# Order of the opening's transposes on TensorE, and of their copies on VectorE, in a fused layer-norm, linear-attention and gated-MLP kernel

## The chip, the cores and the metric

The kernel runs on one core of one Trainium2 chip. The metric is device time in microseconds (us). Where a ratio is given, it is the mean time of one kernel's runs over that of the other's runs of the same rounds, so it is not quite the ratio of the medians beside it.

## The reference, cut to what matters

```python
x = A_x                                   # 2048 x 640, bf16
xn = _layernorm(x, axis=-1)
return x + _A_ref(xn, A_wqkv, A_w_phi, A_wo) + _B_ref(xn, B_w1, B_w3, B_w2)
# _A_ref: q, k, v = xn @ wqkv; softmax feature maps of q and k; kv state; out @ wo
# _B_ref: (silu(xn @ w1) * (xn @ w3)) @ w2
```

Everything starts from the normalized rows xn, and the matmuls of this kernel read them transposed, with the contraction index on the partitions.

## The kernel before

The 2048 rows are 16 tiles of 128. Tiles 0 to 3 are the opening: they are transposed on TensorE (PE), and the later tiles by DMA. For each of the four tiles VectorE (DVE) computes mean and variance and writes a normalized (or, at first, only centered) tile; PE transposes its five 128x128 blocks into one or two PSUM banks; ScalarE (ACT) or DVE copies them to xnT; and PE multiplies xnT by wv (ten matmuls of 320 columns per tile: "V" below).

Tiles 0 and 1 are transposed twice. The first time they are only centered, so that V can start before the variance is known, and ACT multiplies V by the reciprocal standard deviation when it empties the accumulators. The second time they are fully normalized, for all later readers of xnT. Those later readers are first the "gate" matmuls (512 columns, with w1 and w3), which need all four tiles. The start of the first gate matmul is thus the end of the opening.

```python
def T(t, lo, hi, evac, dep, after=()):       # transposes of blocks lo..hi of tile t; cut
    def fn():
        o["ps"] = bank([P, (hi - lo) * P], bf)          # a bank of the ring of six
        for c in range(lo, hi):
            nc.tensor.transpose(o["ps"][:, ...], xn[0][:, t, c * P : (c + 1) * P], ident[:])
    u = plan.op("PE", ...)                   # placed on PE where T() is called
    def evacuate():                          # the copy, placed where the result is called
        XT_of[t] = plan.op(evac, ...)        # "ACT" or "DVE": xnT <- bank
    return evacuate

def V_part(t, cs, o, deps):                  # V of tile t, blocks cs of the contraction; cut
    def fn(cs=cs):
        for c in cs:
            for half in range(2):
                if c == 0:
                    o[half]["ps"] = bank([P, 320], f32)
                nc.tensor.matmul(o[half]["ps"][:], xnT[:, c, ...], wv[:, c, ...], ...)

# the opening, in program order for each engine; cut to its middle
V_part(1, (0, 1), vo[1], [x1[0]])
vo[1]["last"] = V_part(1, (2, 3, 4), vo[1], [x1[1]])
pair_evac(0)                                 # ACT empties V of tile 0
e0 = T(0, 0, KD, "DVE", apply_of[0])         # SECOND transposes of tile 0
e2, e3 = T(2, 0, 2, "ACT", apply2), T(2, 2, KD, "ACT", apply2)
x = [e2(), e3()]                             # ACT copies of tile 2
ln_stats(3); ln_sqrt(3); ln_apply(1, x1); ln_recip(3)
apply3 = ln_apply(3)
e0()                                         # DVE copy of tile 0's second transposes
pair_evac(1)
V_part(2, (0, 1), vo[2], [x[0]])
vo[2]["last"] = V_part(2, (2, 3, 4), vo[2], [x[1]])
e2, e3 = T(3, 0, 2, "DVE", apply3), T(3, 2, KD, "DVE", apply3)
e1 = T(1, 0, KD, "DVE", apply_of[1])         # SECOND transposes of tile 1
x = [e2(), e3()]                             # DVE copies of tile 3
e1()
...
V_part(3, (0, 1), vo[3], [x[0]])
vo[3]["last"] = V_part(3, (2, 3, 4), vo[3], [x[1]])
```

The opening is issued in exactly this order. All that follows is ordered by a list scheduler in Python, from modelled times.

The softmax here doesn't subtract the row's maximum and nothing guards it: scores larger than these inputs give would overflow.

## Time and profile before

| kernel before | value | from |
|---|---|---|
| median time, first 6 runs | 269.78 us (269.22 to 271.86) | times |
| span of the profile | 268.2 us | page |
| PE busy | 262.5 us, 98% | page, part 1 |
| PE's share of the chain that ended last | 95% | page, part 4 |
| first gate matmul starts | 13.743 us | single instructions |

From the page of the kernel before: the span, the busy time of each engine, and the chain of work that ended last by engine.

```profile
span 268.2 us, 5109 instructions
...
PE 262.5 (98%) x1948; PEld 165.2 (62%) x1974; DVE 173.8 (65%) x334; ACT 122.4 (46%) x273; POOL 131.5 (49%) x118
...
PE 95%; DMA 2%; issue 1%; ACTq 0%; ACT 0%; DVE 0%
```

Only PE is nearly always busy, and the chain is made of PE but for a load at the start. Next, the view of who waited for whom, for PE alone, kernel before (waited for: us in total, times, longest us).

```profile
PE bank L227 <- PEq L1094: 0.8, 1, 0.8
PE bank L461 <- ACT xnT L428: 0.3, 1, 0.3
PE bank L461 <- DMA wv<-in_A_wqkv_dram: 0.2, 1, 0.2
```

L461 are the V matmuls, L428 is the ACT copy of transposes. In the whole kernel PE waits for a copy once, for 0.3 us. The PE timeline of the opening, kernel before, shows where (start us, duration us, engine, line, operation, how many, and in brackets the idle time before it):

```profile
9.33 0.72 PE L416 MATMUL bank<-ident,xn 128*128 128x128 bf16 x10
10.35 1.53 PE L461 MATMUL bank<-wv,xnT 128*128 128x320 bf16 x10 [0.30 <-ACT xnT L428]
11.71 0.72 PE L416 MATMUL bank<-ident,xn 128*128 128x128 bf16 x10
12.37 1.53 PE L461 MATMUL bank<-wv,xnT 128*128 128x320 bf16 x10
13.74 1.03 PE L667 MATMUL bank<-xnT,w_107 128*128 128x512 bf16 x3
```

The first line is ten transposes: five second ones of tile 0, then five of tile 2. V of tile 2 follows with the wait. The third line is five transposes of tile 3 and five second ones of tile 1. And this is what ACT and DVE do meanwhile (timelines of ACT and of DVE, kernel before):

```profile
9.92 0.75 ACT L428 COPY xnT<-bank 128x256 bf16<-128x256 bf16 x2 [0.85 <-PE bank L416]
10.55 0.31 ACT L322 ACTIVATE rstd<-mv,eps 128x1 f32<-128x1 f32 x1
```

```profile
10.90 0.16 DVE L333 RECIPROCAL rstd<-rstd 128x1 f32<-128x1 f32 x1 [0.64 <-ACT rstd L322]
11.10 0.45 DVE L352 TENSOR_SCALAR xn<-xg,mv,rstd 128x640 bf16<-128x640 bf16 x1
11.46 1.52 DVE L426 COPY xnT<-bank 128x640 bf16<-128x640 bf16 x4
```

ACT stood idle for 0.85 us until PE brought tile 2's transposes. Behind that copy comes the square root for tile 3 (L322), and behind the root DVE's reciprocal and apply for tile 3: tile 3 hangs on tile 2's copy through ACT's queue. DVE's four copies begin with tile 0's 128x640.

The bracketed waits count from a matmul's end. The Trainium skill, "Perfetto Trace Analysis", § Tensor Engine Instruction, says that the end of a PE instruction in a profile is computed and not observed. Transposes recorded at 0.219 us each start 0.056 us apart, so their recorded ends overlap the next three. All intervals below are therefore from start to start.

### The profile page before, as it was taken

The page shows a single profiled execution, that of the slowest core. Times are in us where ns is not written, and L with a number is a line of the kernel's source. Part 1 is how long each engine was busy: PE and PEld are TensorE (multiplying, and loading weights), DVE is VectorE, ACT ScalarE, POOL GpSimd, SP SyncE. Part 2 cuts the span into 40 slices and gives each one's busy share as a digit, 9 for nine tenths or more (in the row PEclk, how much of TensorE's full clock was granted, in tenths as well). Part 3 has the DMA queues.
Part 4 walks back from the last instruction along what each step waited for, and adds up shares of the span by engine and source line. Part 5 has one row for each costly group of instructions (what it writes and reads, how often), then busy time and mean ns, then how long its engine had stood idle before and what let it go on. Part 6 is the DMA issues. An engine that isn't in the chain of part 4 may idle for free.

```text
span 268.2 us, 5109 instructions
## 1 busy us (share of the span) xinstructions
PE 262.5 (98%) x1948; PEld 165.2 (62%) x1974; DVE 173.8 (65%) x334; ACT 122.4 (46%) x273; POOL 131.5 (49%) x118
## 2 busy tenths in 40 slices
PE   8999999999999999999999999999999999999995
PEld 3645555555565666666555677765765665657774
DVE  4738798777665996876997748766367366443221
ACT  3756676657676676767545222234225213120000
POOL 3263679975557577699315715443542553112000
PEclk9999999999999999999999999999999999999999
DMA  7999939200440027528295457495913937430401
GB/s 214 311 275 289 261 116 302 79 0 0 119 78 0 2 86 202 127 108 130 92 282 191 130 141 194 143 263 191 217 43 122 228 115 210 122 80 22 124 25 49
DMA packets 69528, 38.10 MB, mean 142 GB/s; under 512 B 49664, under 2 KB 67456, under 8 KB 69504
## 3 DMA queue, kind: packets, MB, share of 16 engines
q1 hardware_dynamic: 68784, 37.18, 50.7%
q10 hardware_dynamic: 720, 0.61, 0.7%
q8 instruction: 15, 0.25, 0.4%
q14 instruction: 9, 0.07, 0.1%
HBM read 12.81 MB, written 12.98 MB: 96 GB/s over the span
## 4 chain that ended last, share of the span: by engine, by line
PE 95%; DMA 2%; issue 1%; ACTq 0%; ACT 0%; DVE 0%
PE bank L667 38%; PE bank L447 22%; PE bank L832 19%; PE bank L845 8%; PE rtbank L742 2%; PE bank L461 2%; DMA wv<-in_A_wqkv_dram 2%; PE bank L620 1%; PE kva L592 1%; PE kvb L592 1%; PE bank L416 0%; ACTq L175 0%; ACT xnT L428 0%; ACTq L183 0%; DVE res L859 0%
## 5 line engine op out<-in xcount | busy, mean ns | idle before, releaser
L711 POOL TENSOR_TENSOR hT<-gs,up 128x512 bf16<-128x512 bf16 x43 | 49.7, 1157 | 81.3 <-ACT up L706 42.2
L667 PE MATMUL bank<-xnT,w_108 128*128 128x512 bf16 x235 | 59.2, 379 | 0.3
L667 PE MATMUL bank<-xnT,w_107 128*128 128x512 bf16 x219 | 58.2, 379 | 1.1
L832 PE MATMUL bank<-w_109,hT 128*128 128x320 bf16 (+2 forms) x396 | 55.1, 295 | 0.0
L447 PEld LDWEIGHTS <-xnT 128*128 128x128 bf16 x440 | 42.1, 98 | 17.6
L832 PEld LDWEIGHTS <-hT 128*128 128x128 bf16 x396 | 37.9, 98 | 15.2
L683 ACT ACTIVATE th<-bank 128x512 bf16<-128x512 f32 x48 | 28.7, 597 | 39.8 <-PE bank L667 39.1
L688 DVE SCALAR_TENSOR_TENSOR gs<-th,bank 128x512 bf16<-128x512 bf16 x48 | 32.9, 685 | 20.6 <-ACT th L683 20.0
L667 PEld LDWEIGHTS <-w_108 128*128 128x128 bf16 x240 | 23.5, 98 | 28.3
L859 DVE TENSOR_TENSOR res<-bank,xr 128x320 bf16<-128x320 f32 (+2 forms) x33 | 15.8, 478 | 38.6 <-PE bank L845 38.6
L706 ACT ACTIVATE up<-bank 128x512 bf16<-128x512 f32 x43 | 25.7, 597 | 22.5 <-PE bank L667 22.5
L667 PEld LDWEIGHTS <-w_107 128*128 128x128 bf16 x240 | 22.4, 98 | 20.9
L845 PE MATMUL bank<-wo,oT 128*128 128x320 bf16 (+2 forms) x165 | 24.7, 295 | 0.0
L447 PE MATMUL bank<-wkphi,xnT 128*128 128x320 bf16 x160 | 24.3, 299 | 0.0
L447 PE MATMUL bank<-wqphi,xnT 128*128 128x320 bf16 x160 | 24.3, 299 | 0.0
L845 PEld LDWEIGHTS <-oT 128*128 128x128 bf16 x165 | 15.8, 98 | 5.8
L447 PE MATMUL bank<-wv,xnT 128*128 128x320 bf16 x120 | 18.3, 299 | 0.0
L519 ACT ACTIVATE exp_128<-bank 128x320 bf16<-128x320 f32 x32 | 11.5, 435 | 13.6 <-PE bank L447 13.6
L519 ACT ACTIVATE exp_131<-bank 128x320 bf16<-128x320 f32 x32 | 11.5, 437 | 12.2 <-PE bank L447 12.2
L519 ACT ACTIVATE exp_129<-bank 128x320 bf16<-128x320 f32 x32 | 11.5, 435 | 10.7 <-PE bank L447 10.7
L519 ACT ACTIVATE exp_130<-bank 128x320 bf16<-128x320 f32 x32 | 11.5, 439 | 10.1 <-PE bank L447 10.1
L297 DVE BATCH_NORM_STATS2 stats<-xg 128x6 f32<-128x320 bf16 x32 | 13.7, 470 | 2.5 <-DMA xg<-in_A_x_dram 2.5
(141 smaller groups left out, 294.6 us busy)
## 6 DMA issues: line engine op xcount, KB each, us to landing
xr<-in_A_x_dram SPq DMA_DIRECT2D x4, 640.0 KB, 5.7
out_dram<-res SPq DMA_DIRECT2D x15, 160.0 KB, 1.8
w_107<-in_B_w_dram SPq DMA_DIRECT2D x4, 480.0 KB, 6.2
w_108<-in_B_w_dram SPq DMA_DIRECT2D x4, 480.0 KB, 6.8
w_109<-in_B_w_dram SPq DMA_DIRECT2D x1, 1920.0 KB, 8.4
xg<-in_A_x_dram SPq DMA_DIRECT2D x11, 160.0 KB, 3.7
wo<-in_A_wo_dram SPq DMA_DIRECT2D x1, 800.0 KB, 5.4
xg<-in_A_x_dram SPq DMA_DIRECT2D x1, 640.0 KB, 5.1
```

The lines of the kernel that those rows point to most:

```text
L297: nc.vector.bn_stats(out=stats[:, t, h, :], in_=xg[c][:, i, h * 320 : (h + 1) * 320])
L447: nc.tensor.matmul(o["ps"][:], xnT[:, c, t * P : (t + 1) * P], w[:, c, 320 * half : 320 * half + 320], start=(c == 0), stop=(c == KD - 1),)
L461: nc.tensor.matmul(o[half]["ps"][:], xnT[:, c, t * P : (t + 1) * P], wv[:, c, 320 * half : 320 * half + 320], start=(c == 0), stop=(c == K ...
L519: nc.scalar.activation(out=box["e"][:, sgn, 16 * half : 16 * half + 16, :], in_=o["ps"][:].rearrange("p (h d) -> p h d", d=Dh), func=AF.Ex ...
L667: nc.tensor.matmul(o["ps"][:], w[:, k, fi * P : (fi + 1) * P], xs[:, k, :], start=(k == 0), stop=(k == KD - 1))
L683: nc.scalar.activation(out=box["th"][:], in_=og["ps"][:], func=AF.Tanh, scale=0.5)
L688: nc.vector.scalar_tensor_tensor(out=box["gs"][:], in0=box["th"][:], scalar=1.0, in1=og["ps"][:], op0=ALU.add, op1=ALU.mult)
L706: nc.scalar.activation(out=box["up"][:], in_=ou["ps"][:], func=AF.Copy, scale=0.5)
L711: lambda: nc.gpsimd.tensor_mul(out=hT[c][:, fi, :], in0=box["gs"][:], in1=box["up"][:]),
L832: nc.tensor.matmul(o["ps"][:], hT[c][:, fi, ti * P : (ti + 1) * P], w2[:, fi, lo:hi], start=(fi == 0), stop=False,)
L845: nc.tensor.matmul(o["ps"][:], oT[c][:, k, ti * P : (ti + 1) * P], wo_of[0][:, k, lo:hi], start=False, stop=(k == KD - 1),)
L859: nc.vector.tensor_tensor(out=box["res"][:, lo:hi], in0=o["ps"][:], in1=xr[c][:, ti, lo:hi], op=ALU.add)
```

## The change

Tile 2's transposes are to reach ACT sooner, so they go ahead of tile 0's second ones, which nobody needs before the gate matmuls. For the same reason DVE's copy of the latter goes behind tile 3's copies.

```diff
     pair_evac(0)
+    e2, e3 = T(2, 0, 2, "ACT", apply2), T(2, 2, KD, "ACT", apply2)
     e0 = T(0, 0, KD, "DVE", apply_of[0])
-    e2, e3 = T(2, 0, 2, "ACT", apply2), T(2, 2, KD, "ACT", apply2)
     x = [e2(), e3()]
@@
     apply3 = ln_apply(3)
-    e0()
     pair_evac(1)
@@
     x = [e2(), e3()]
+    e0()
     e1()
```

## The prediction

> **What bounds the kernel.** TensorE. The page shows PE busy 262.5 of 268.2 us (98%); the chain of waits is 95% PE. The view of who waited for whom has, for PE, only 0.8 us at the start, 0.2 us for wv near 6.6 us, and 0.3 us at 10.35 us, where the third tile's V matmuls wait for the ScalarE copy of its transposes. After about 13 us the timeline shows no PE wait, so what the opening gains should reach the end unchanged.
>
> **What changes.** No instruction is added or removed. (a) On PE the five second transposes of tile 0 go behind tile 2's five. (b) On VectorE their 128x640 copy goes behind the two copies for tile 3.
>
> **Costs, from start times of single instructions.** Transposes start 0.056 us apart, V matmuls 0.136 us. Before: tile 0's second transposes start at 9.325, tile 2's at 9.604 and 9.660, then 9.716 to 9.828. The ScalarE copy starts at 9.916 (0.256 us after its last transpose's start), takes 0.373 us, and V of tile 2 starts at 10.344. PE was free at about 9.885: a gap of 0.46 us by starts, which the waits view gives as 0.30, as it counts from the matmul's end. The Trainium skill, "Perfetto Trace Analysis", § Tensor Engine Instruction, says those ends are estimated; hence I use starts.
>
> After: tile 2's first two transposes at 9.325 and 9.381 (their input was ready at 8.91), copy from 9.637 to 10.010, V of tile 2 from about 10.065: 0.28 us earlier. About 0.18 us of the gap stays. The second copy ends at about 10.39, soon enough for the fifth matmul.
>
> Tile 3 follows: Sqrt on ScalarE starts 0.28 us earlier, so reciprocal and apply do (apply ends near 11.26, not 11.54), and tile 3's transposes start at 11.43 (before 11.712). Before, the first tile 3 copy started 0.256 us after its transpose, so it waited for PE and not for tile 0's copy: (b) alone should give nothing. Copy 11.75 to 12.04, V of tile 3 at 12.09 (before 12.373), still behind a gap of 0.10 us. The moved copies end at about 12.70 and 13.10; the gate matmuls that need them start at about 13.46. One risk: if tile 3's second V accumulator gets the PSUM bank of tile 3's second transposes, its first matmul waits for that copy (to 12.30), and 0.1 us of the gain is lost.
>
> **On the critical path:** 0.17 to 0.28 us, all in the gap before V of tile 2. Loads do not eat it: the first gate weights landed at 9.39 and 11.16, the transposed K weights at 18.56 for a use at 20.2.
>
> **Predicted time:** 269.55 us, range 268.9 to 270.2 (8 in 10). Within 2%: 0.98; faster by over 2%: 0.01; slower: 0.01. The effect is smaller than the spread of the runs before (269.22 to 271.86).
>
> **Right if:** in the timeline tile 2's transposes are ahead of tile 0's, first copy near 9.64, V of tile 2 at 10.06, tile 3's transposes at 11.43, first gate matmul at 13.46 to 13.58 instead of 13.742, the span shorter by as much. Wrong if V of tile 3 still starts at 12.37 or later, or PE waits for VectorE copies as it did not before.
>
> **What would make it wrong.** The later order comes from a list scheduler whose modelled times start with the opening, so orders on VectorE, ScalarE, POOL or the queues may change later and a PE wait of some tenths appear or go; PSUM banks are dealt in order of release, and the moved copy holds one for longer; loads could come just too late for an earlier PE.

## The result

| | before | changed |
|---|---|---|
| median | 269.62 us (20 runs, 269.22 to 271.86) | 269.50 us (10 runs, 268.91 to 270.49) |
| ratio | | 0.9991, 95% interval 0.9969 to 1.0013 |

This is within the predicted range, and within 2%; by time alone the interval does not tell the change from nothing, and without the two runs of 271.84 and 271.86 us of the kernel before the ratio would be about 1.000 (an estimate from the recorded times). From the page of the changed kernel, the same parts as before:

```profile
span 267.3 us, 5109 instructions
...
PE 262.1 (98%) x1948; PEld 164.7 (62%) x1974; DVE 173.7 (65%) x334; ACT 122.3 (46%) x273; POOL 131.5 (49%) x118
...
PE 98%; issue 1%; DVE 0%
```

Who waited for whom, PE alone, changed kernel. Neither V wait is listed any more. By starts, the one for ACT has not gone but shrunk, from 0.46 to 0.18 us, and V of tile 0 still went on only when blocks of wv had landed (below); the view counts from recorded ends and misses both:

```profile
PE bank L227 <- PEq L1094: 0.8, 1, 0.8
```

The timeline of PE, then of ACT and DVE, changed kernel:

```profile
8.55 0.72 PE L416 MATMUL bank<-ident,xn 128*128 128x128 bf16 x10
9.28 1.53 PE L461 MATMUL bank<-wv,xnT 128*128 128x320 bf16 x10
10.65 0.72 PE L416 MATMUL bank<-ident,xn 128*128 128x128 bf16 x10
11.31 1.64 PE L461 MATMUL bank<-wv,xnT 128*128 128x320 bf16 x10
12.79 1.24 PE L667 MATMUL bank<-xnT,w_107 128*128 128x512 bf16 x4
```

```profile
8.86 0.76 ACT L428 COPY xnT<-bank 128x256 bf16<-128x256 bf16 x2 [0.56 <-PE bank L416]
9.50 0.31 ACT L322 ACTIVATE rstd<-mv,eps 128x1 f32<-128x1 f32 x1
```

```profile
9.84 0.16 DVE L333 RECIPROCAL rstd<-rstd 128x1 f32<-128x1 f32 x1 [0.35 <-ACT rstd L322]
10.04 0.45 DVE L352 TENSOR_SCALAR xn<-xg,mv,rstd 128x640 bf16<-128x640 bf16 x1
10.97 1.35 DVE L426 COPY xnT<-bank 128x256 bf16<-128x256 bf16 x4 [0.49 <-PE bank L416]
```

Three things are to be seen. First, transposes to V of tile 2: 8.55 to 9.28 is 0.73 us, before it was 1.02. Second, the V group of tile 3 lasts 1.64 us instead of 1.53: something inside it holds. Third, everything is earlier by more than the change can explain: already the transposes at the top start at 8.55 and not at 9.33, 0.78 us earlier, and no instruction of PE ahead of them was touched.

Which engine's order did change? A comparison of the two built programs, instruction by instruction, gave no difference on ACT, POOL and SP; on DVE only the place of one 128x640 copy. On PE, where groups of transposes from one line are told apart by the place in xn that they read, only tile 2's five transposes and their weight loads have moved. The later part, which the list scheduler orders, came out the same.

### Reading both traces from a common event

The first V matmul of tile 1 comes before anything that was moved. From it, with starts of single instructions, in us (the last two columns are absolute: its own start, and the time from the first gate matmul to the kernel's last matmul):

| profile | tile 2's transposes¹ | V of tile 2 | tile 3's transposes | V of tile 3 | V of tile 3, 1st to 2nd matmul | first gate matmul | its own start | gate to last |
|---|---|---|---|---|---|---|---|---|
| before | 1.358 | 2.377 | 3.745 | 4.406 | 0.146 | 5.775 | 7.968 | 251.370 |
| changed | 1.358 | 2.096 | 3.465 | 4.125 | 0.261 | 5.606 | 7.188 | 251.377 |

¹ the first of the ten transposes, in the kernel before one of tile 0's.

So V of tile 2 gains 0.281 us and tile 3 keeps it (0.280, 0.281); then 0.115 us are lost between the first and the second V matmul of tile 3, and 0.169 us reach the first gate matmul. From there on both kernels take the same time to 7 ns. The rest of the difference between the two spans (0.9 us) is the start of the first V matmul of tile 1, and that hangs on loads: in the kernel before the fourth block of wv landed at 7.39 us and V of tile 0 went on at 7.43; in the changed kernel at 6.42 and 6.46, where the fifth block then cost 0.19 us more.

What released tile 3's transposes? In both traces they start 0.135 or 0.136 us after the last V matmul of tile 2, the spacing of V matmuls: PE's own order released them. The apply of tile 3 on DVE had ended 0.17 us earlier each time (3.574 and 3.292 us after the common event). The step through ACT's queue was still needed. Had the apply stayed at 3.574, the transposes could not have started before about 3.63, with the 0.057 us from apply to transpose that is measured below (an estimate; no run separates this step).

### The profile page after: what moved, and what is told of

Same layout as the page of the kernel before. It is cut to its first block, busy times and chain, and to the rows that moved or that the text cites. A ratio compares the mean times of both kernels' runs of the same rounds, so it can differ in the third digit from the quotient of the medians.

```text
span 267.3 us, 5109 instructions
## 1 busy us (share of the span) xinstructions
PE 262.1 (98%) x1948; PEld 164.7 (62%) x1974; DVE 173.7 (65%) x334; ACT 122.3 (46%) x273; POOL 131.5 (49%) x118
## 4 chain that ended last, share of the span: by engine, by line
PE 98%; issue 1%; DVE 0%
PE bank L667 38%; PE bank L447 22%; PE bank L832 20%; PE bank L845 8%; PE bank L461 2%; PE rtbank L742 2%; PE bank L227 1%; PE bank L620 1%; PE kva L592 1%; PE kvb L592 1%; PE bank L416 1%; DVE res L859 0%
```

## The experiments

My theory had three parts. (1) The gain comes from the order on PE alone, through ACT's copy of tile 2 and, behind it in ACT's queue, the root for tile 3. (2) The moved DVE copy gives nothing and costs 0.115 us: with the copies in the new order, the second V accumulator of tile 3 is given the PSUM bank that tile 3's second group of transposes has just left, and waits for its copy. (3) Nothing after the opening absorbs or adds anything. Rivals: the copy order helps tile 3; the 0.9 us of the span is the change; the opening is partly hidden behind later loads.

For (2), this is how the built programs deal out the six banks, from tile 2's transposes on (order of PE, bank numbers):

```
before:   T0' 2  T2a 5  T2b 3  V2 1,5  T3a 3  T3b 0  T1' 4  V3 2,3
changed:  T2a 2  T2b 5  T0' 3  V2 1,2  T3a 5  T3b 0  T1' 4  V3 5,0   <- 0 is T3b's
```

T3a and T3b are the two groups of tile 3's transposes, T0' and T1' the second transposes of tiles 0 and 1. Before, the two V accumulators of tile 3 took the banks of T0' and T3a; now they take those of T3a and T3b. V of tile 3 needs T3a's copy anyway, but T3b's ends about 0.26 us later.

### A second and a third profile of both kernels

Edits: none. before_again is the kernel of before, after_again and after_third are the changed one.

> The kernel of before once more, for a second profile. My theory: first V matmul of tile 1 to first gate matmul 5.775 us again, first gate matmul to the last matmul the same within 0.1 us, while the start of the first V matmul of tile 1 may differ by up to 1 us with the landing of the loads. Rival: the interval itself varies by tenths from profile to profile, then differences of 0.17 us between kernels mean nothing.

> The changed kernel once more, for a second profile. My theory: from the first V matmul of tile 1 to the first gate matmul 5.61 us (before: 5.775 us), whatever the span of the profile is. The 0.9 us by which the first profile of the changed kernel was shorter in span (267.3 against 268.2 us) is mostly the moment at which the wv load landed, 0.78 us earlier before any changed instruction ran, and not the change. Rival: the change itself is worth 0.9 us, then the interval or the span shows it again. Ratio 0.999 to 1.0.

> The changed kernel a third time, for its ratio beside the one above. My theory: 0.17 us shorter than before in the opening, ratio 0.9994, which five rounds can't tell from 1; first V of tile 1 to first gate matmul 5.61 to 5.64 us again. Rival: a ratio clearly off 1 with the interval unchanged would mean that the time is made elsewhere.

| profile | V of tile 2 | V of tile 3 | 1st to 2nd | first gate | own start | gate to last |
|---|---|---|---|---|---|---|
| before_again | 2.377 | 4.407 | 0.146 | 5.775 | 7.242 | 251.374 |
| after_again | 2.128 | 4.158 | 0.259 | 5.637 | 7.504 | 251.376 |
| after_third | 2.097 | 4.127 | 0.260 | 5.607 | 7.325 | 251.371 |

Times: after_again 269.62 us median, ratio 1.0012 (0.9984 to 1.0040); after_third 269.37 us, ratio 0.9991 (0.9957 to 1.0025); before_again one run of 269.21 us. Without the runs at clock 0.993 and 0.994 the two ratios would be about 0.9999 and 0.9998 (an estimate from the recorded times). The span of before_again was 267.5 us, shorter than that of after_again (267.6).

The interval of the opening repeats to the nanosecond in the kernel before, while its start differs by 0.73 us. The rival that the change is worth 0.9 us falls: the kernel before reaches the same span when its loads land early. The timelines of PE for the two profiles of the kernel before, at the loads: first the first one, then before_again.

```profile
6.58 0.43 PE L461 MATMUL bank<-wv,xnT 128*128 128x320 bf16 x2 [0.20 <-DMA wv<-in_A_wqkv_dram]
6.85 0.44 PE L416 MATMUL bank<-ident,xn 128*128 128x128 bf16 x5
```

```profile
6.01 0.45 PE L416 MATMUL bank<-ident,xn 128*128 128x128 bf16 x5
6.70 2.06 PE L461 MATMUL bank<-wv,xnT 128*128 128x320 bf16 x14 [0.23 <-DMA wv<-in_A_wqkv_dram]
```

The same five transposes (tile 1's) are 0.84 us apart in two executions of one program.

after_again is 0.03 us longer than the other two profiles of the changed kernel. There the apply of tile 2 on DVE ended 1.322 us after the first V matmul of tile 1 (1.255 and 0.950 in the others), and tile 2's transposes started at 1.379 instead of 1.358: they waited for DVE. In the kernel before, tile 0's second transposes stood at this place, whose input was ready 0.7 us sooner (0.651 against 1.349 us in before_again). So the change uses up a reserve against DVE.

### pe_only: the order on PE alone

```diff
     pair_evac(0)
+    e2, e3 = T(2, 0, 2, "ACT", apply2), T(2, 2, KD, "ACT", apply2)
     e0 = T(0, 0, KD, "DVE", apply_of[0])
-    e2, e3 = T(2, 0, 2, "ACT", apply2), T(2, 2, KD, "ACT", apply2)
```

> Part (a) alone: tile 2's transposes ahead of tile 0's second ones on PE, VectorE's copies in the order of before. My theory: all of the gain comes from here and part (b) gives 0.115 us of it back, through the PSUM bank of tile 3's second V accumulator. So: V of tile 2 0.28 us earlier, V of tile 3 0.28 us earlier, no wait before the second V matmul of tile 3 (0.146 us after the first, not 0.26), first V matmul of tile 1 to first gate matmul 5.50 us (before 5.775, changed 5.61). Rival: the moved copies are needed for tile 3 to start early; then V of tile 3 starts later than in the changed kernel.

Measured: V of tile 2 at 2.097, V of tile 3 at 4.128, 0.146 us to its second matmul, first gate matmul at 5.496: 0.279 us less than before, all as expected. From the timeline of PE (pe_only), V of tile 3 lasts 1.53 us, as in the kernel before:

```profile
11.82 1.53 PE L461 MATMUL bank<-wv,xnT 128*128 128x320 bf16 x10
13.19 1.67 PE L667 MATMUL bank<-xnT,w 128*128 128x512 bf16 x6
```

Time: 269.56 us median, ratio 1.0005 (0.9978 to 1.0033), with one run of 271.63 among six, at clock 0.994; without it the ratio would be about 0.9990 (an estimate from the recorded times). The time can't show it; the trace does.

### copies_only: the order of DVE's copies alone

```diff
     apply3 = ln_apply(3)
-    e0()
     pair_evac(1)
@@
     x = [e2(), e3()]
+    e0()
     e1()
```

> Part (b) alone: PE order of before, VectorE's copy of tile 0's second transposes behind tile 3's copies. My theory: V of tile 2 does not move, V of tile 3 does not start earlier, and the second V matmul of tile 3 comes 0.26 us instead of 0.146 us after the first, since it waits for the copy of tile 3's second transposes: first V of tile 1 to first gate matmul 5.89 us, 0.115 us longer than before. Rival: the copies' order is what sped tile 3 up; then the interval is shorter than 5.775 us.

Measured: V of tile 2 at 2.378 and of tile 3 at 4.409, both as before; 0.259 us to its second matmul; first gate matmul at 5.887, 0.112 us later than before. The timeline of PE (copies_only) has the long V group of tile 3 again, and the 0.30 us wait that part (a) removes:

```profile
9.83 1.53 PE L461 MATMUL bank<-wv,xnT 128*128 128x320 bf16 x10 [0.30 <-ACT xnT L428]
11.20 0.72 PE L416 MATMUL bank<-ident,xn 128*128 128x128 bf16 x10
11.87 1.64 PE L461 MATMUL bank<-wv,xnT 128*128 128x320 bf16 x10
```

Time: 269.59 us, ratio 0.9997 (0.9983 to 1.0012). In the traces the two parts add up: -0.279 + 0.112 = -0.167 us, against -0.169 for both together.

### halves: the same bank, asked for later

In the changed kernel, tile 3's first four V matmuls do both contraction blocks of the first accumulator and then both of the second. The banks stay those of the changed kernel (5 and 0).

```diff
-            for c in cs:
-                for half in range(2):
+            if t == 3 and cs == (0, 1):
+                order = [(0, 0), (1, 0), (0, 1), (1, 1)]
+            else:
+                order = [(c, half) for c in cs for half in range(2)]
+            if True:
+                for c, half in order:
```

> The changed kernel with one edit: tile 3's first four V matmuls do both contraction chunks of the first half and then both of the second half, so the second accumulator is first written 0.27 us after the first and not 0.14. My theory: the wait for its bank (0.115 us) goes; first V of tile 1 to first gate matmul 5.50 us instead of 5.61. Rival: the 0.26 us between the first two V matmuls of tile 3 has another cause than the bank, and shows up before the third or in the same place: 5.61 us.

Measured: 0.146 us to the second matmul, which is now of the same accumulator, and 0.136 us from there to the third, the first of the second accumulator; first gate matmul at 5.506. The wait has gone and has not come back further on: V of tile 3 to first gate is 1.368 us, as in the kernel before (1.369), against 1.481 in the changed one. In the changed kernel the record fits the bank too: DVE's copy of T3b ended at 11.522 us and the held matmul started at 11.574. The timeline of PE (halves) has V of tile 3 at 1.53 us again:

```profile
12.30 1.53 PE L465 MATMUL bank<-wv,xnT 128*128 128x320 bf16 x10
```

Time: 269.70 us, ratio 0.9996 (0.9983 to 1.0009).

The Trainium skill, "Perfetto Trace Analysis", § Matmuls, advises to let independent matmul groups rotate through different PSUM banks so that the emptying of one overlaps the next. This case shows the limit of a ring: which bank comes next follows from the order in which the copies free them, and moving one copy made a group draw a bank that was still being emptied.

### delay16: does the opening reach the end?

In the kernel before, 16 matmuls of 512 columns with constant operands stand between V of tile 3 and the first gate matmul. Their planned duration is zero, so that the list scheduler orders the rest as before.

```diff
+    def idle_work():
+        ps = bank([P, 512], f32)
+        for _ in range(16):
+            nc.tensor.matmul(ps[:], nc.const_aps.tensor(1.0, [P, P], bf), nc.const_aps.tensor(1.0, [P, 512], bf))
+    plan.op("PE", 0.0, idle_work)
```

> The kernel of before with 16 extra matmuls of 512 columns (constant operands, a bank of their own, nobody reads them) between V of tile 3 and the first gate matmul: 16 times 0.2157 is 3.45 us of PE work. My theory: after the opening PE never waits, so 3.4 to 3.5 us reach the end: ratio 1.0128. Rival: loads or another engine set the pace later and the opening is hidden in part; then under 2.5 us reach the end.

Measured: the first gate matmul came at 9.275 instead of 5.775, 3.500 us later (the extra matmuls started 0.219 us apart, not 0.2157), and from it to the last matmul took 251.371 us. Time: 273.15 against 269.83 us, ratio 1.0119 (1.0101 to 1.0137), that is 2.7 to 3.7 us. No part of a later opening is hidden. The timeline of PE (delay16):

```profile
13.72 3.66 PE L973 MATMUL bank<-const-bfloat16-1.0 128*128 128x512 bf16 x16
17.22 2.10 PE L667 MATMUL bank<-xnT,w 128*128 128x512 bf16 x9
```

What remains open is the other direction far beyond these sizes: an opening some microseconds shorter might meet the loads.

### no_gaps: both groups of transposes earlier still

The changed kernel leaves 0.18 us before V of tile 2 and 0.10 us before V of tile 3. Here the transposes of tiles 2 and 3 also go ahead of the last two V matmuls of the tile before:

```diff
-    vo[1]["last"] = V_part(1, (2, 3, 4), vo[1], [x1[1]])
-    pair_evac(0)
+    V_part(1, (2, 3), vo[1], [x1[1]])
     e2, e3 = T(2, 0, 2, "ACT", apply2), T(2, 2, KD, "ACT", apply2)
+    vo[1]["last"] = V_part(1, (4,), vo[1], [])
+    pair_evac(0)
@@
-    vo[2]["last"] = V_part(2, (2, 3, 4), vo[2], [x[1]])
+    V_part(2, (2, 3), vo[2], [x[1]])
     e2, e3 = T(3, 0, 2, "DVE", apply3), T(3, 2, KD, "DVE", apply3)
+    vo[2]["last"] = V_part(2, (4,), vo[2], [])
```

> The changed kernel with tile 2's transposes also ahead of the last two V matmuls of tile 1, and tile 3's ahead of the last two of tile 2, so that more PE work hides each copy. My theory: the gap before V of tile 2 (0.18 us left in the changed kernel) falls to 0, the one before V of tile 3 and the bank wait (0.10 and 0.115 us) to about 0.05 in all: first V of tile 1 to first gate matmul 5.25 to 5.30 us (changed 5.61, before 5.775), and the time 0.4 to 0.5 us below the one before, ratio about 0.998. Rival: the splits of the V groups cost PE time themselves, or the apply of tile 3 is not ready; then PE waits for VectorE and the interval stays near 5.6 us.

> The version that looked fastest, once more, for a second ratio and a second profile. My theory: first V of tile 1 to first gate matmul between 5.25 us (apply of tile 2 ready in time) and 5.6 us (not ready), and PE gaps before tile 2's and tile 3's transposes that end when VectorE's apply does; ratio 0.998 to 0.999 again. Rival: the first ratio of 0.9984 was luck; then 1.000.

The first interval was a miss: 5.578 us where 5.25 to 5.30 were expected. The gaps before V of tiles 2 and 3 did close, but PE now waits before the transposes. The timelines of PE's weight loads (a transpose loads the tile as its weights) and of DVE, no_gaps:

```profile
8.51 0.28 PEld L416 LDWEIGHTS <-xn 128*128 128x128 bf16 x5 [0.42 <-DVE xn L352]
```

```profile
8.01 0.45 DVE L352 TENSOR_SCALAR xn<-xg,mv,rstd 128x640 bf16<-128x640 bf16 x1
```

The apply of tile 2 ended at 8.46, and tile 2's transposes began at 8.51. Where transposes waited for an apply, they started 0.057 or 0.058 us after its end: tile 2's and tile 3's in no_gaps, tile 2's in after_again above, and tile 3's in no_gaps_again. My estimate had taken the apply's end from the first profile of the kernel before (0.939 us after the first V of tile 1), in which PE had waited for wv while DVE went on; here it was 1.277.

The trace kept under no_gaps_again is of none of the timed runs (span 269.5 us; theirs were 267.1 to 268.0). It gives 5.754 us, with the apply long ready (0.530) but PE at half rate in the first V matmuls of tile 1, for a reason that comes at the end of the next section. These matmuls start up to 0.267 us apart instead of 0.136 and lose 0.47 us; without that the interval is 5.28, inside the 5.25 to 5.30 that were expected with the apply in time.

Times: 269.35 us, ratio 0.9984 (0.9971 to 0.9997), and 269.33 us, ratio 0.9983 (0.9963 to 1.0002).

### t2_early: pe_only, with tile 2's transposes earlier still

The order on PE alone (no moved copy, hence no bank wait), plus the first half of the edit above:

```diff
-    vo[1]["last"] = V_part(1, (2, 3, 4), vo[1], [x1[1]])
+    V_part(1, (2, 3), vo[1], [x1[1]])
+    e2, e3 = T(2, 0, 2, "ACT", apply2), T(2, 2, KD, "ACT", apply2)
+    vo[1]["last"] = V_part(1, (4,), vo[1], [])
     pair_evac(0)
     e0 = T(0, 0, KD, "DVE", apply_of[0])
-    e2, e3 = T(2, 0, 2, "ACT", apply2), T(2, 2, KD, "ACT", apply2)
```

> Part (a) alone, and tile 2's transposes also ahead of the last two V matmuls of tile 1; tile 3 as in part (a) alone. My theory after the first miss: the next thing that binds is VectorE's chain (statistics of tile 2, apply), which follows the landing of x. Where the apply of tile 2 ends before the tenth V matmul of tile 1 could start, the interval from first V of tile 1 to first gate matmul is 5.32 us (changed 5.61, part (a) alone 5.50); where it ends later, tile 2's transposes wait for VectorE by the difference and the interval is up to 5.6 us. The wait before the second V matmul of tile 3 is not there. Ratio near 0.998. Rival: moving the transposes into V of tile 1 costs PE time by itself; then the interval is 5.6 us although the apply was ready.

> The version with tile 2's transposes ahead of the last two V matmuls of tile 1, once more, beside the changed kernel on the same chip. My theory from the traces (0.32 us less than before in the interval that the order can reach, 251.37 us after it in every profile): ratio near 0.9988, so 0.9972 of the first time was partly luck. First V of tile 1 to first gate matmul: 4.2 us plus the end of tile 2's apply, counted from first V of tile 1, where that is over 1.03 us. Rival: the version is worth 0.7 us by something that the opening's interval does not hold; then 0.997 again.

Measured in the first profile: 5.46 us to the first gate matmul, with the apply at 1.17 (0.32 us less than before); V of tile 3 lasts 1.53 us, so there is no bank wait. The first gate matmul came at 12.89; the fifth V matmul of tile 1 came at 7.97, so by the spacing of 0.136 us the first came at 7.43; and the apply ended at 8.60:

```profile
7.97 0.71 PE L461 MATMUL bank<-wv,xnT 128*128 128x320 bf16 x4
8.66 0.45 PE L416 MATMUL bank<-ident,xn 128*128 128x128 bf16 x5
11.52 1.53 PE L461 MATMUL bank<-wv,xnT 128*128 128x320 bf16 x10
12.89 1.89 PE L667 MATMUL bank<-xnT,w 128*128 128x512 bf16 x7
```

Times: 268.89 against 269.59 us, ratio 0.9972 (0.9951 to 0.9994); repeated, 269.19 against 269.60 us, ratio 0.9988 (0.9952 to 1.0025). The 0.9988 that was expected came out, but partly by luck: without the run at clock 0.994 on this side and the one at 0.993 on the other it would be about 0.9984 (an estimate from the recorded times).

Its second profile fell on one of the four executions at a lower clock (271.48 us; the other five took 268.89 to 269.50). The view of who waited for whom and a line of the timeline, PE alone, and the granted clock of PE by fortieths of the span (in tenths), t2_early_again:

```profile
PE bank L461 <- DMA wv<-in_A_wqkv_dram: 1.3, 2, 1.1
```

```profile
6.95 1.22 PE L461 MATMUL bank<-wv,xnT 128*128 128x320 bf16 x4 [1.15 <-DMA wv<-in_A_wqkv_dram]
```

```profile
PEclk9799999999999999999999999999999999999999
```

The loads came so late that PE idled, and then the clock record has PE at half rate from 7.00 to 10.41 us: four V matmuls of tile 1 start up to 0.267 us apart instead of 0.136. They lose 0.42 us (3 x 0.131 + 0.03), so the 5.729 us of this profile are 5.31 without it, and 5.32 was expected where the apply is in time (it was: 0.529). The Trainium skill, "TensorE: Matmul & The Clock Gate", § Part 1, says that the clock falls to half after an idle window of about 3.4 us and names gaps over 3.4 us as the danger. Here the half-rate stretch was 3.41 us long, as a window of that length would make it, but the longest single PE wait of the profile was 1.1 us: no gap of 3.4 us was needed. In the 3.41 us before that stretch, PE's records cover 0.50 of the time.

The traces kept under t2_early (span 269.6 us, again of none of the timed runs) and no_gaps_again look alike: PE waited 1.0 and 0.7 us for wv at about 6 us, V matmuls started 0.267 us apart, and the clock record has the full rate only from 10.02 and 10.22 us, where the other traces with a clock record have it from 3.6 to 6.8 us. In this trace of t2_early the interval is 5.493 with the apply at 0.524; less the 0.19 us that the half rate cost, it is 5.30. So the three kept traces of these two versions with the apply in time (5.28, 5.30 and 5.31) give about what was expected, once the half rate is taken off. That the waits for wv brought on the half rate is what the order in time suggests; no experiment tests it.

## Why the prediction was right

- **The bound.** Right. The view lists no wait of PE after the opening; the time from the first gate matmul to the last matmul was 251.370 to 251.390 us in all 13 profiles, and an added 3.50 us arrived whole.
- **V of tile 2 earlier by 0.28 us.** Right: 0.281. Tile 3 kept it: 0.280 and 0.281. The step through ACT's queue took place (the apply of tile 3 ended 0.282 us earlier), but it made room and did not set the pace: PE's own order released tile 3's transposes.
- **"(b) alone should give nothing."** Half right. It does not speed up tile 3, but it is not free: it costs 0.112 us. The prediction named this cost as a risk, with its mechanism (the bank of tile 3's second transposes) and its size (0.1 us); it did not see that the moved copy itself is what brings it about. The built programs, which exist before any run, show the bank.
- **0.17 to 0.28 us on the critical path.** Right, at the low end: 0.169 and 0.168 us in two profiles and 0.138 in the one where the apply of tile 2 was late.
- **269.55 us.** 269.50 was measured, but this agreement is luck. The prediction took 0.23 us off a median of six runs; with 20 runs that median was 269.62, and the three ratios of the changed kernel (0.9991, 1.0012, 0.9991) do not tell 0.17 us from zero. What is shown is the interval in the traces, not the total.
- **The times by which it was to be judged.** Wrong in form. It gave absolute starts (V of tile 2 at 10.06, first gate matmul at 13.46 to 13.58) and "the span shorter by as much". They came at 9.28 and 12.79, and the span was 0.9 us shorter. The landing of wv moves the whole opening: the first V of tile 1 started between 7.18 and 8.17 us in ten of the kept traces, and at 9.26 to 9.65 in the three with half rate in V of tile 1. Counted from the common event, as if it had come at 7.968 again, the same starts are 10.06 and 13.57, with tile 3's transposes at 11.43 and V of tile 3 at 12.09: each is as predicted, the first gate matmul at the late end of its range because the bank risk came true.
- **"Their input was ready at 8.91."** True of that profile, but taken as a reserve of 0.42 us that the kernel does not have: it was 0.06 us, the bare latency, in after_again.

What the unresolved total hides can be seen in the profiled runs: the device time less the absolute start of the first gate matmul was 256.19 us in both profiles of the kernel before (269.93 - 13.743 and 269.21 - 13.017), and 256.20, 256.22 and 256.19 in the three of the changed kernel. The scatter of the runs is, in these, all made before the first gate matmul.

t2_early and no_gaps had lower medians than both kernels in all four of their timings, and one interval of each excludes 1. Which of the two is better was not settled, nor was the first 0.7 us of t2_early: the trace accounts for 0.3 of it.

## What to carry to other kernels

For a change worth less than the scatter, take the interval from an event ahead of the change to an event behind it, by instruction starts, and ask of the rest only that it stays the same; spans and absolute times compare the landing of loads. When copies out of PSUM change places, write down which bank each later group will draw: a copy that nobody waits for can still decide who waits. And before work is moved forward, look for the input's reserve in more than one profile, since a profile in which PE was held up by a load can show another engine with more time than it has.

## What the Trainium skill lacked or had wrong

- "TensorE: Matmul & The Clock Gate", § Part 4 (PE-mode transpose), puts a 128x128 bf16 transpose at about 390 ns alone and 275 ns in a kernel. Here it was recorded at 219 ns, and in a row they started 56 ns apart, at the full rate; what counts for placing them is the 56.
- The same page, § Part 1, warns of PE gaps over about 3.4 us. In t2_early_again the clock was halved from 7.00 to 10.41 us although the longest single PE wait was 1.1 us. The page does tell of a kernel whose clock swung under many short idles, but gives no share of a window that is enough; in the 3.41 us before this stretch PE's records cover 0.50.
- No page gives the whole time from a transpose to the matmul that reads it through PSUM and a copy. Here: last transpose's start to copy's start 0.256 us, copy 0.373 us (128x256 on ACT) or 0.292 us (on DVE), copy's end to the matmul's start 0.05 us, about 0.6 to 0.7 us in all; from a DVE apply's end to the first transpose that reads it 0.057 or 0.058 us.
- "Perfetto Trace Analysis", § Matmuls, on rotating PSUM banks does not say that in a ring dealt by order of release the place of an unrelated copy decides the bank: 0.112 us here for one moved copy.
